# The unread matmuls of steps 8 to 20 in the chunk loop of a fused mLSTM and MoE kernel

## The chip, the core and the metric

The kernel runs on one core of one Trainium2 chip. The metric is the device time in microseconds (us); three runs of the kernel before gave 218.23, 218.18 and 217.78 us, median 218.18. The profile shown is of one further execution; its span, from the first to the last instruction, is 217.2 us.

Five engines work side by side. TensorE (PE in the profile; its weight loads are PEld) multiplies matrices into PSUM, VectorE (DVE), ScalarE (ACT) and GpSimd (POOL) do the rest of the arithmetic, and SyncE (SP) issues transfers. The clock of TensorE is granted by the chip and may fall to a half; the profile gives the granted share as PEclk.

## What is computed

Two stages, one behind the other. First an mLSTM cell over 4 x 8 heads, 768 time steps and a head size of 40. Then the result, 3072 rows of 320, goes through a mixture of 8 experts with one expert for each row.

```python
# stage 1, for each time step t
m_new = np.maximum(f_gate[:, :, t] + m, i_gate[:, :, t])
f_stab = np.exp(f_gate[:, :, t] + m - m_new)
i_stab = np.exp(i_gate[:, :, t] - m_new)
C = f_stab * C + i_stab * np.einsum('bhd,bhe->bhde', vt, kt)   # [..., None, None] cut
n = f_stab * n + i_stab * kt
h_tilde = np.einsum('bhde,bhe->bhd', C, qt)
denom = np.maximum(np.abs(np.einsum('bhd,bhd->bh', n, qt)), 1.0)
y[:, :, t] = sigmoid(o_gate[:, :, t]) * h_tilde / denom         # sigmoid written out in the reference

# stage 2, x: (3072, 320)
logits = x @ w_gate
expert_idx = np.argmax(logits, axis=1)
gate_w = probs[np.arange(N), expert_idx]                        # probs: softmax of logits
# rows sorted by expert; for each expert e
h = np.maximum(x_sorted[lo:hi] @ w1[e], 0.0)
y_sorted[lo:hi] = h @ w2[e]
out = gate_w[:, None] * y_sorted[inv_perm]
```

## The kernel before

The kernel turns the recurrence of stage 1 into chunks of 128 time steps: 4 batches of 6 chunks make NT = 24 steps of one loop, called the chunk loop here. While it runs, the rows that are done go through the gate of stage 2, are given a place and are sent to an array in HBM that is sorted by expert. Behind the loop the experts' multiplications run.

The order of instructions on each engine is the order of the program. One step of the loop, cut to the calls that matter:

```python
for s in range(-3, NT):
    P, odd = (s - 4) // 2, s % 2
    do(scores, s + 1)            # TensorE: scores of the next chunk
    do(transposes, s + 2)        # TensorE: k and q of the chunk after it
    ...
    do(values, s + 2)
    ...                          # a send; in even steps gate(P)
    do(states, s)                # TensorE: state times q, update of the state
    do(load, s + 6 if s >= -1 else -1)
    ...                          # in even steps rank(P, s - 1); warm(3) in the last
    do(xtrans, s - 1)            # TensorE: rows transposed for the gate
    do(ogate, s + 2)
    do(attend, s)                # TensorE: scores times values
    ...                          # place, keep_rows
    do(rows, s)                  # VectorE and GpSimd: x of this chunk
    if odd and 0 <= (s - 3) // 2:
        logits((s - 3) // 2, s - 1)      # TensorE: gate logits of two chunks
        choose((s - 3) // 2)             # VectorE: the expert of each row
        count((s - 3) // 2)
    ...                          # a send, a part of the constants, weight loads near the end
```

The change is in `scores`. Its s is the loop's step plus one. For each pair of heads there is one matmul into sA and one into sB; VectorE masks sA into dA, ScalarE copies sB to dB, GpSimd masks dB.

```python
def scores(s):
    d = st[s]
    kb, qb = d["kb"], d["qb"]
    sA = ps1.tile([128, PR, 128], F32, name="sA")
    sB = ps1.tile([128, PR, 128], F32, name="sB")
    for _ in range(3 if 1 <= s < 8 or s > NT - 4 else s % 2):
        nc.tensor.matmul(
            sA[:].rearrange("p j t -> p (j t)"), lhsT=ident_b[:],
            rhs=st[s - 1]["dA"][:].rearrange("p j t -> p (j t)"), start=True, stop=True,
        )
    for j in range(PR):
        nc.tensor.matmul(sA[:, j, :], lhsT=kb[0:D, j, :], rhs=qb[0:D, j, :], start=True, stop=True)
        nc.tensor.matmul(
            sB[:, j, :], lhsT=kb[DP : DP + D, j, :], rhs=qb[DP : DP + D, j, :], start=True, stop=True,
        )
    d["dA"] = chk.tile([128, PR, 128], BF16, name="dA")
    nc.vector.tensor_tensor(d["dA"][:], sA[:], cmask[:, None, :].to_broadcast([128, PR, 128]), op=ALU.mult)
    d["dB"] = chk.tile([128, PR, 128], BF16, name="dB")
    nc.scalar.copy(d["dB"][:], sB[:])
    ...                          # GpSimd: the lower half of dB to zero
```

The loop at the top of it issues matmuls whose result nobody reads: the identity times dA of the step before, 512 columns, into sA, which the score matmuls then overwrite. There are three of them in each of the s from 1 to 7 and from 21 to 23, and s % 2 in between. `warm` does the same into a tile named junk around the end of the loop.

The gate logits stand at the end of an odd step, so right ahead of the unread matmul of the next `scores`:

```python
def logits(P, host, c0=0):
    ...
    for i, t in enumerate(r["t"]):           # two chunks
        for db in range(DB):                 # three blocks of 128
            nc.tensor.matmul(
                lg[:, i * E : (i + 1) * E], lhsT=st[t]["xT"][:, db * 128 : (db + 1) * 128],
                rhs=wg_sb[:, db, :], ...     # E = 8 columns
            )
```

Behind the loop come `layer1` and `layer2` of the experts (hp and zp in the profile), their rows sent by GpSimd to the output (`out_dram`), with weights (`w_all`) that GpSimd's queue loads from HBM.

Of the kernel before, what the change touches and what calls it, by code (L numbers as in the profile page):

```python
# [19 lines left out]
def kernel(  # L20
# [22 lines left out]
    NT = N // 128  # L43
# [263 lines left out]
    with tc.tile_pool(name="ring", bufs=1) as ring_pool, \  # L307
# [67 lines left out]
        def scores(s):  # L375
            d = st[s]
            kb, qb = d["kb"], d["qb"]
            sA = ps1.tile([128, PR, 128], F32, name="sA")
            sB = ps1.tile([128, PR, 128], F32, name="sB")
            for _ in range(3 if 1 <= s < 8 or s > NT - 4 else s % 2):  # L380
                nc.tensor.matmul(  # L381
                    sA[:].rearrange("p j t -> p (j t)"), lhsT=ident_b[:],
                    rhs=st[s - 1]["dA"][:].rearrange("p j t -> p (j t)"), start=True, stop=True,
# [10 lines that stand above are left out]
            nc.gpsimd.affine_select(  # L394
                d["dB"][:], d["dB"][:], compare_op=ALU.is_ge, fill=0.0,
                base=0, pattern=[[0, PR], [1, 128]], channel_multiplier=-1,
            )
# [209 lines left out]
        for s in range(-3, NT):  # L607
            P, odd = (s - 4) // 2, s % 2
            last = s == NT - 1
            do(scores, s + 1)  # L610
            do(transposes, s + 2)
            if s == -3:
# [266 lines left out]
```

## Time and profile before

| What | Before |
|---|---|
| Time, median of three | 218.18 us |
| Span of the profiled execution | 217.2 us |
| Mean granted clock of TensorE | 0.984 |
| Chain that ended last, by engine | PE 46%, POOL 20%, issue 14%, DVE 9%, DMA 5%, ACT 3% |
| Line 381, all unread matmuls of `scores`, in the trace | 28 of 128x512 |
| Scores of the last chunk start | 110.6 us |

A row of a group or a timeline names the line of the kernel, the engine, the operation, what is written and read (out<-in) and the shape. In the chain of work that ended last, each row has a start in us, the time for which this piece held the chain, and the piece; "issue" there is time in which the engine waited for nothing that the profile shows. In the slices of the page each digit stands for one of 40 equal parts of the span, in tenths of busy time, or for PEclk in tenths of the full clock.

Some matmul records can be missing from a trace, and the ends of matmuls are modelled: a duration of one matmul is a latency which overlaps with its neighbours.

### The profile page before, as it was taken

Reading aid. Unit: us, or ns where it says so; the run is one execution under the profiler, and the core shown is the slowest. Engines: PE = TensorE matmul, PEld = TensorE weight load, DVE = VectorE, ACT = ScalarE, POOL = GpSimd, SP = SyncE. Lnnn points to the kernel's source line nnn. Section 1 sums busy time; section 2 is a strip of 40 time slices with the busy share of each in tenths; the row PEclk is TensorE's granted clock in tenths of the full one; section 3 lists DMA queues with packets and bytes.
Section 4 is the critical chain, followed back from the end, with each engine's and each line's share of the span. In section 5 each row is a group of like instructions: output and inputs, shape, how many; then the busy total and the mean of one; then the engine's idle time right before and its main releaser. Section 6 shows DMA issues by size and latency. Waiting matters only on the chain.

```text
span 217.2 us, 5727 instructions
## 1 busy us (share of the span) xinstructions
PE 192.3 (89%) x2048; PEld 151.8 (70%) x2057; DVE 124.8 (57%) x410; ACT 117.3 (54%) x273; POOL 139.3 (64%) x238
## 2 busy tenths in 40 slices
PE   1299999999999999979899998969999986999970
PEld 1168788899998899978786755647667654676740
DVE  7746667677787878797776342345833332333320
ACT  2458657797789897896751552323333322332330
POOL 6036786644869889749999489838656786253221
PEclk9999999999999999999998899999999999999996
DMA  7999999989999989994799999999999999985310
GB/s 139 197 198 190 205 205 204 231 156 254 178 193 173 195 161 206 193 204 84 142 184 262 222 205 150 193 254 233 216 229 245 231 290 408 409 317 201 149 46 10
DMA packets 120782, 44.32 MB, mean 204 GB/s; under 512 B 102506, under 2 KB 115821, under 8 KB 120752
## 3 DMA queue, kind: packets, MB, share of 16 engines
q1 hardware_dynamic: 105456, 25.34, 55.9%
q0 software_dynamic: 14832, 18.38, 40.3%
q8 instruction: 17, 0.28, 0.5%
q10 hardware_dynamic: 464, 0.21, 0.4%
q14 instruction: 13, 0.11, 0.2%
HBM read 39.30 MB, written 9.37 MB: 224 GB/s over the span
## 4 chain that ended last, share of the span: by engine, by line
PE 46%; POOL 20%; issue 14%; DVE 9%; DMA 5%; ACT 3%; POOLq 1%; ACTq 0%; DVEq 0%
POOL out_dram L287 7%; PE hp L474 6%; PE zp L280 5%; DMA w_all<-in_moe_w_dram 5%; PE hp L406 5%; PE tk L368 4%; POOL x_sorted L579 4%; PE dC L414 4%; PE hp L267 4%; PE tq L368 3%; PE xt L451 3%; PE sA L386 3%; PE sA L381 2%; POOL x_sb L444 2%; POOL rest L297 2%
## 5 line engine op out<-in xcount | busy, mean ns | idle before, releaser
L273 DVE TENSOR_SCALAR h<-hp 128x512 bf16<-128x512 f32 x25 | 17.3, 692 | 40.6 <-PE hp L267 26.3
L287 POOL DMA_INDIRECT out_dram<-zo,s_idx x20 | 20.0, 1002 | 16.3 <-ACT zo L285 10.0
L275 ACT ACTIVATE h<-hp 128x512 bf16<-128x512 f32 x25 | 14.9, 597 | 25.2 <-PE hp L267 19.9
L579 POOL DMA_INDIRECT x_sorted<-x_all,slots x24 | 25.3, 1054 | 4.9 <-issue 3.9
L444 POOL TENSOR_TENSOR x_sb<-x_sb,den 128x320 f32<-128x320 f32 x23 | 16.8, 729 | 17.2 <-DVE den L442 17.1
L280 PE MATMUL zp<-w_all,h 128*128 128x320 bf16 x160 | 24.5, 300 | 3.5 <-DMA w_all<-in_moe_w_dram 1.6
L280 PEld LDWEIGHTS <-h 128*128 128x128 bf16 x200 | 17.7, 98 | 13.2 <-DVE h L273 2.7
L285 ACT COPY zo<-zp 128x320 f32<-128x320 f32 x25 | 10.7, 426 | 27.2 <-PE zp L280 23.7
L267 PEld LDWEIGHTS <-w_all 128*128 128x128 bf16 x256 | 18.4, 98 | 5.6 <-issue 3.4
L393 ACT CAST dB<-sB 128x512 bf16<-128x512 f32 x24 | 14.0, 585 | 13.7 <-PE sB L387 11.5
L267 PE MATMUL hp<-xT,w_all 128*128 128x128 bf16 (+1 forms) x224 | 21.1, 243 | 0.0
L406 PE MATMUL hp<-C_sb,qT 104*128 104x82 f32 x160 | 20.7, 272 | 0.0
L368 PE MATMUL tk<-ident,kq 128*104 128x128 f32 x96 | 16.4, 296 | 4.2 <-DMA kq<-in_k_dram 4.2
L406 PEld LDWEIGHTS hp<-C_sb,qT 104*128 104x128 f32 x160 | 19.4, 192 | 0.3
L453 ACT COPY xT<-xt 128x384 f32<-128x384 f32 x24 | 11.6, 482 | 13.5 <-PE xt L451 12.5
L356 POOL CAST vAb<-vA 128x328 bf16<-128x328 f32 x24 | 11.0, 459 | 11.7 <-DVE vA L354 11.7
L474 PE MATMUL hp<-wg_sb,xT 128*128 128x8 f32 x144 | 18.0, 258 | 0.0
L414 PE MATMUL dC<-vA,kq 128*104 128x82 f32 x160 | 17.9, 254 | 0.0
L394 POOL TENSOR_SCALAR_AFFINE_SELECT dB<-dB 128x512 bf16<-128x512 bf16 x24 | 16.5, 689 | 1.7 <-ACT dB L393 1.5
L474 PEld LDWEIGHTS hp<-wg_sb,xT 128*128 128x128 f32 x144 | 17.4, 195 | 0.1
L391 DVE TENSOR_TENSOR dA<-sA,cmask 128x512 bf16<-128x512 f32 x24 | 16.0, 669 | 1.4 <-PE sB L387 1.4
L414 PEld LDWEIGHTS dC<-vA,kq 128*104 128x104 f32 x160 | 16.3, 172 | 0.0
(160 smaller groups left out, 455.8 us busy)
## 6 DMA issues: line engine op xcount, KB each, us to landing
wx<-w_all SPq DMA_DIRECT2D x10, 640.0 KB
w_all<-in_moe_w_dram POOLq DMA_DIRECT2D x8, 640.0 KB
w_all<-in_moe_w_dram POOLq DMA_DIRECT2D x8, 512.0 KB
kq<-in_k_dram SPq DMA_DIRECT2D x24, 160.0 KB
kq<-in_q_dram SPq DMA_DIRECT2D x24, 160.0 KB
v<-in_v_dram SPq DMA_DIRECT2D x24, 160.0 KB
o_sb<-in_o_gate_dram SPq DMA_DIRECT2D x24, 160.0 KB
x_sorted<-zrow POOLq DMA_DIRECT2D x8, 241.5 KB
```

The source lines that it names most:

```text
L267: nc.tensor.matmul(hp[:, i, :], lhsT=w[:, c : c + 128], rhs=xT[:, db, :], start=False, stop=(db == FL - 1), skip_group_check=True,)
L273: nc.vector.tensor_relu(dst, hp)
L280: nc.tensor.matmul(zp, lhsT=g["h"][:, fb, j * 128 : (j + 1) * 128], rhs=g["w"][1][:, fb, :], start=(fb == 0), stop=(fb == FB - 1),)
L287: ins = nc.gpsimd.indirect_dma_start(out=out[:, :], out_offset=bass.IndirectOffsetOnAxis(ap=at, axis=0), in_=zo, in_offset=None, bounds_ch ...
L368: nc.tensor.transpose(tp[:, j, :], two(d[n], j), ident[:])
L391: nc.vector.tensor_tensor(d["dA"][:], sA[:], cmask[:, None, :].to_broadcast([128, PR, 128]), op=ALU.mult)
L394: nc.gpsimd.affine_select(d["dB"][:], d["dB"][:], compare_op=ALU.is_ge, fill=0.0, base=0, pattern=[[0, PR], [1, 128]], channel_multiplier=-1,)
L406: nc.tensor.matmul(hp[:, 2 * j * D1 : (2 * j + 2) * D1], lhsT=d["qT"][:, j, :], rhs=st["C"][:, j].rearrange("p h d -> p (h d)"), start=(j ...
L414: nc.tensor.matmul(st["dC"][:, j], lhsT=two(d["k"], j), rhs=d["vA"][:, 2 * j : 2 * j + 2, :], start=(c == 0 and j == 0), stop=True, skip_g ...
L444: eng.tensor_tensor(x3d, x3d, den[:].unsqueeze(2).to_broadcast([128, H, D]), op=ALU.mult)
L474: nc.tensor.matmul(lg[:, i * E : (i + 1) * E], lhsT=st[t]["xT"][:, db * 128 : (db + 1) * 128], rhs=wg_sb[:, db, :], start=(fresh and i == ...
L579: ins = nc.gpsimd.indirect_dma_start(out=xs[:, :], out_offset=bass.IndirectOffsetOnAxis(ap=slots[:, t : t + 1], axis=0), in_=x_all[:, t, : ...
```

## The change

In the steps from s = 8 to s = 20, `scores` issues no unread matmul any more; before, it issued one where s is odd. The three of each earlier and later step stay, and so does `warm`. The unread matmuls have no part in the result. They keep TensorE occupied[...]; the change takes out those for which the loop's own work is to do that.

```diff
             sA = ps1.tile([128, PR, 128], F32, name="sA")
             sB = ps1.tile([128, PR, 128], F32, name="sB")
-            for _ in range(3 if 1 <= s < 8 or s > NT - 4 else s % 2):
+            for _ in range(3 if 1 <= s < 8 or s > NT - 4 else 0):
                 nc.tensor.matmul(
                     sA[:].rearrange("p j t -> p (j t)"), lhsT=ident_b[:],
                     rhs=st[s - 1]["dA"][:].rearrange("p j t -> p (j t)"), start=True, stop=True,
```

## The prediction

> **What bounds the kernel now.** I read the page first (busy shares, the slices, the chain that ended last), then the instructions of line 381, then the chain and the timeline of TensorE around each of the matmuls that go away. The page says that TensorE is the busiest engine, and the slices say where.
>
> ```profile
> PE 192.3 (89%) x2048; PEld 151.8 (70%) x2057; DVE 124.8 (57%) x410; ACT 117.3 (54%) x273; POOL 139.3 (64%) x238
> ...
> PE   1299999999999999979899998969999986999970
> ...
> PEclk9999999999999999999998899999999999999996
> ```
>
> One slice is 5.43 us. The chunk loop lies in slices 2 to 21, and TensorE is at nine tenths or more in nearly all of them until about 92 us, at full clock. So a matmul taken out of that stretch should shorten it, unless another engine sets the pace at that place. The clock row dips around slices 21 and 22 only.
>
> Which matmuls go? `scores(s)` runs one step ahead of the loop's counter. Before, its s from 8 to 20 gave s % 2 unread matmuls, so one each for s = 9, 11, 13, 15, 17, 19: six in all. The instructions of line 381 between 44 and 93 us are these six (the first row is their weight load):
>
> ```profile
> L381 PEld LDWEIGHTS <-ident_b x6: 181/181/181, 49.2 to 90.4; 128*128 128x128 bf16 x6
> L381 PE MATMUL sA<-dA,ident_b x6: 376/376/377, 49.3 to 90.5; 128*128 128x512 bf16 x6
> ```
>
> The 376 ns are a latency: they overlap with neighbours. What one costs on the path is read from the chain of work that ended last. At 82 us:
>
> ```profile
> 81.31 1.33 PE hp L474 x12
> 82.64 0.23 PE sA L381
> 82.87 0.16 PE sA L386
> ```
>
> The unread matmul holds the chain for 0.23 us. The chain shows the same 0.23 at 49.48, 58.07, 74.06 and 90.62 us. At 66 us it is different: there the chain leaves TensorE at the end of the gate logits and goes over VectorE.
>
> ```profile
> 64.59 1.34 PE hp L474 x12
> 65.94 0.02 issue
> 65.96 0.19 DVE lgs L484
> ...
> 66.98 0.43 DVE cums L498
> ...
> 67.62 0.60 DVE dA L391
> ```
>
> VectorE chooses experts until 67.62 us and only then makes dA, though its scores were in PSUM before 66.4 us. The unread matmul at 65.78 is in the shadow of that work.
>
> [...] the clock is half from 118.08 to 121.49 us (3.41 us) and falls again at 213.64, which is 28.0 windows after 118.08. [...] TensorE was busy for 3.05 us of the window before the fall.
> [...]
>
> So the six matmuls are there for the clock, not for a result: they stand right behind the twelve gate-logits matmuls (128 x 8 each, 1.33 us), which stream few columns.
>
> **The change, part by part.** It removes six weight loads and six 128x512 matmuls, and adds nothing. Apart from names, the instruction order of the engines stays. The wait for VectorE's last read of sA, which the unread matmul carried, moves to the first score weight load, beside its wait for kb on ScalarE: the form that the steps without an unread matmul have already.
> - Saving per place, a second way: with the unread matmul the first score matmul ends at 49.87 us, 0.39 after the last logits matmul (49.48). Where no unread matmul stands ahead of the scores (53.22 us), the first score matmul ends at 53.44, 0.16 after the matmul ahead of it (53.28). The difference is 0.23 us again.
> - On the path: five places, 5 x 0.23 = 1.15 us. The sixth, at 65.78, saves 0 by my reading (0.23 if I am wrong).
> - Does the saving last? Behind 90.62 us the chain goes over ACT (dB, 91.30), DVE and POOL, all started by these scores, so it moves with them. From 97.6 to 115 us it is POOL, which sends rows and issues weight loads one behind another (18.19 us busy in the 20 us from 96 to 116). That row of work begins with an x_sb at 96.71 that waited for the earlier chain, so it starts earlier too. Then comes the longest wait of all:
>
> ```profile
> 131.26 0.70 POOL w_all L178
> 131.96 1.00 POOL w_all L183 x2
> ...
> 133.01 11.71 DMA w_all<-in_moe_w_dram
> ```
>
>   The transfers queue up behind those issued earlier. But in 100 to 104 us the DMA engines are busy for only 0.38, so the queue that makes this wait begins after that, with issues from POOL's row, and moves with it. I count the whole 1.15 us through to the end.
> - Sum without a clock effect: 218.18 - 1.15 = 217.03 us.
>
> **The rivals.**
>
> *The clock falls.* This is the real danger, since the matmuls are there to prevent it. To judge it I counted streamed columns in each 3.41 us window as the trace has them: every matmul but transposes, f32 columns counted four times, a matmul across an edge by its part[...]. Counting f32 four times is my choice; counted once, a window that kept its clock (70.29 to 73.70) would lie below one that lost it. Two windows were followed by a fall: 114.66 to 118.08, and the last with matmuls in it, 210.24 to 213.65. Their non-transpose groups:
>
> ```profile
> L474 PE MATMUL hp<-wg_sb,xT 128*128 128x8 f32 x12 | 1.5, 256 | 0.0
> L567 PE MATMUL junk<-dA,ident_b 128*128 128x512 bf16 x2 | 0.9, 440 | 0.0
> ```
>
>   With eight 41-column matmuls and 0.8 of an unread one inside, the first has 384 + 328 + about 400 columns, 0.14. The last has 5.3 matmuls of 320 columns, 0.21. Both fell. The windows that kept the clock in the chunk loop have 0.34 and more; one of the lowest, 80.53 to 83.94, has 0.35 with one unread matmul (0.06) in it, so about 0.29 without. Sliding the window over the trace from 40 to 92 us[...] the lowest share is 0.27 before, and 0.24 with the six taken out and what follows pulled forward. The other minima move up as often as down, for what is pulled forward into the window is f32 work. So the limit is somewhere from 0.21 to 0.34, and the change moves the worst place by 0.03. [...] At 120.88 us twelve logits matmuls with 0.61 us of their time at half clock took 1.70 us instead of 1.49, a third of the slow time lost, so about 1.2 us for a whole window. One fall would cancel the gain (218.2), two would make 219.4. For it speaks the purpose of the lines; against it, that steps without an unread matmul keep the full clock already (70.29 to 73.70 has eleven of twelve logits matmuls and none of line 381). I give one extra fall or more a quarter.
>
> *Another engine paces those steps.* If VectorE, ScalarE or GpSimd were the bound at more of the places, as at 66 us, the gain would shrink to 0.5 us or less (217.7). From 76 to 92 us GpSimd is busy for about 1.8 of each 2 us, so it is near. Against it: the chain itself passes through line 381 at five of six places.
>
> *The transfer hides it.* If the 11.71 us wait for w_all ended by the DMA queue's own work, begun early, the end would not move: 218.1. The idle DMA time at 100 to 104 speaks against it. One chance in ten.
>
> **Range and chances.** 217.0 with three chances in five, something from 217.5 to 218.2 where part of it is hidden or one fall happens, and about 219 with two falls: I put the middle at 217.1 us. The three times before span 0.45 us, which I add below, and a fall with a little scatter above: 216.3 to 218.7. A gain of 2% would need 4.4 us, more than the six matmuls' whole latency (2.3 us); a loss of 2% would need at least four falls. Chances: faster by over 2% 0.01, within 2% 0.97, slower by over 2% 0.02.
>
> **What would show it right or wrong.** In the profile after: no line 381 from 44 to 93 us; the first score matmul ends 0.16 us after the last logits matmul, not 0.39; the logits groups in the loop start 0.23 us earlier per place, except over the one at 66 us, and by 90 us by about 0.9 us in all; GpSimd's row of sends and the wait for w_all start 1.1 us earlier. A half-clock stretch between 40 and 100 us, with 1.2 us lost behind it, proves the clock rival; a loop that ends earlier while the multiplications of the experts start no earlier proves the transfer rival. I am wrong altogether if the time rises without a fall of the clock.

## The result and the profile after

The changed kernel took 0.9941 of the time before (95% interval 0.9916 to 0.9967): on a median of 218.03 us before, that is 1.3 us less (0.7 to 1.8), with executions at 216.54 and 216.92 us. This ratio, like those below, leaves out executions that lie more than about 1.5% above the fastest of the same kernel: here two of the four, at 222.95 and 221.82 us with a mean TensorE clock of 0.945 instead of 0.975. By an estimate from clock and span, 2 x (1 - 0.945) x 221.2 us, the longer of the two spent 24 us at half clock, 14 more than the one at 216.54 us. That is four windows of 3.41 us more, at 1.6 us each; no trace shows where they lay.

The page of the changed kernel, in the rows that were shown of the one before:

```profile
PE 193.0 (90%) x2051; PEld 153.2 (71%) x2051; DVE 125.5 (58%) x410; ACT 117.5 (55%) x273; POOL 138.8 (65%) x238
...
PE   1289999999999899999998999898999999999970
...
PEclk9999999999999999969999699999999999999996
```

TensorE is as full as before, and the clock row has a second dip, in the slice that begins at 91 us. The stretches around it say how long it was:

```profile
core 0: us, PE busy (x) PEld busy (x) DVE busy (x) ACT busy (x) POOL busy (x), PEclk, DMA share, GB/s
88.41:91.82 3.41, 3.18 (x39) 2.89 (x39) 2.46 (x9) 2.77 (x7) 3.23 (x6) 1.00 0.84 153
91.82:95.24 3.42, 3.42 (x28) 3.33 (x27) 2.90 (x10) 2.64 (x9) 2.34 (x5) 0.50 1.11 205
```

One window of 3.41 us at half clock, right behind the scores that once had an unread matmul ahead of them (s = 19). "Window" here and below is the spacing that the two profiles show: from the first full clock to the last fall it changes only after whole multiples of 3.413 us. It was full for 102.40 and 92.16 us in the profile before (30 and 27 windows) and for 75.09, 23.89 and 88.75 us in the one after (22, 7 and 26), and half for one window at each fall between them. The chain at the place near 66 us, of which the prediction said that VectorE paced it:

```profile
64.58 1.33 PE hp L474 x12
65.91 0.16 PE sA L386
...
66.36 0.58 ACT dB L393
66.94 0.49 ACT kb L370
67.43 0.49 ACT qb L370
67.92 0.49 ACT qT L373
68.41 0.58 ACT gex L513 x4
...
69.01 0.17 DVE gsum L517
```

No line 381 stands between logits and scores any more. And it is ScalarE, started by these scores, on whose last piece (gex) VectorE waits.

These two profiles don't show where the gain comes from. The spans are 217.2 and 214.7 us, yet the copies of the first expert rows (lines 285, 273) run later in the one after, by 1.4 us: its full clock began at 16.73 us instead of 15.68, it lost 0.9 us at one tq transpose (70.64 us) and it had the window above. Near the loop's end it also waited for a load of the output gate, which landed 9.55 us after its issue, where none in the profile before took over 5.2 us:

```profile
101.60 9.55 DMA o_sb<-in_o_gate_dram
```

ScalarE stood still for the last 1.7 us of it, and by the last steps of the loop this cost 0.8 us (measured on x_sb against the second profile of the change, below: 1.70 us later ahead of the wait, 2.50 behind it). The lead of the profile after comes from 176 us on, where in the profile before TensorE stood still for reasons that the trace doesn't name:

```profile
177.22 2.20 PE L280 MATMUL zp<-w_all,h 128*128 128x320 bf16 x14 [0.80 <-issue]
...
181.66 0.22 PE L242 MATMUL tp<-ident_b,x_all 128*64 128x128 bf16 x1 [0.48 <-issue]
182.60 0.27 PE L239 MATMUL tp<-ident_b,x_all 128*128 128x128 bf16 x2 [0.72 <-issue]
```

The change touches nothing there. A pair of profiles without such accidents comes first among the experiments.

### The profile page after: what moved, and what is told of

Its sections match the earlier page's. It is cut to its first block, busy times and chain, and to the rows that moved or that the text cites. A ratio compares the mean times of both kernels' runs of the same rounds, so it can differ in the third digit from the quotient of the medians.

```text
span 214.7 us, 5730 instructions
## 1 busy us (share of the span) xinstructions
PE 193.0 (90%) x2051; PEld 153.2 (71%) x2051; DVE 125.5 (58%) x410; ACT 117.5 (55%) x273; POOL 138.8 (65%) x238
## 4 chain that ended last, share of the span: by engine, by line
PE 62%; DVE 10%; issue 9%; POOL 7%; ACT 5%; DMA 4%; POOLq 0%; DVEq 0%; ACTq 0%
PE zp L280 9%; PE hp L267 8%; PE hp L474 7%; PE hp L406 5%; PE dC L414 5%; DMA o_sb<-in_o_gate_dram 4%; PE tk L368 4%; POOL out_dram L287 4%; PE tq L368 4%; PE xt L451 4%; PE hp L258 3%; PE sA L386 3%; PE sA L381 3%; PE hp L280 2%; PE hp L426 2%
## 5 line engine op out<-in xcount | busy, mean ns | idle before, releaser
L414 PE MATMUL dC<-vA,kq 128*104 128x82 f32 x160 | 18.5, 261 | 0.0
L414 PEld LDWEIGHTS dC<-vA,kq 128*104 128x104 f32 x160 | 17.1, 178 | 0.0
```

The costliest lines, as they stand in the source:

```text
L414: nc.tensor.matmul(st["dC"][:, j], lhsT=two(d["k"], j), rhs=d["vA"][:, 2 * j : 2 * j + 2, :], start=(c == 0 and j == 0), stop=True, skip_g ...
```

## The experiments

They ran on three chips, in groups: the first four kernels, the next four, the last four. The kernel before ran beside each group, with medians of 216.24, 222.81 and 224.70 us, so ratios are compared and not times. Ratios are to the kernel before on the same chip. "Path theory" below means that the six matmuls leave the path and nothing else happens; "clock theory", that they hold the clock, and that windows at half clock come where they go.

### The kernel before again, and the change again

No edit in the first; the second is the change itself.

> The kernel before, unchanged, as a measure of what changes without any change. Clock theory (the unread matmuls hold the clock): every execution near 218.0 us, mean granted clock 0.98, at most one half-clock window between 16 and 211 us. Chance theory (windows at half clock fall to either kernel alike): some executions at a mean clock of 0.95 and 221 us here too.

> The changed kernel again. Path theory (six matmuls of 0.23 us leave the path, nothing else): 216.6 us, mean clock as before, 0.98. Clock theory: the executions differ with the number of half-clock windows, about 1.5 us for each: near 216.7 us at a mean clock of 0.975 and near 222 us at 0.945, and the trace shows half-clock windows between 40 and 100 us.

Measured: ratios 0.9996 (0.9964 to 1.0029) and 0.9934 (0.9899 to 0.9969). Neither trace has a half-clock window between 17 and 146 us, so here the two loops can be laid side by side. The shift of ScalarE's copy of sB into dB, which follows at once on the scores, against the kernel before (0.12 us of earlier start taken off):

| Place | s = 9 | 11 | 13 | 15 | 17 | 19 |
|---|---|---|---|---|---|---|
| Shift of dB, us | -0.23 | -0.46 | -0.70 | -0.93 | -1.16 | -1.18 |

The rows of s = 13, of the kernel before and of the changed one:

```profile
67.15 0.59 ACT L393 CAST dB<-sB 128x512 bf16<-128x512 f32 x1 [0.47 <-PE sB L387]
66.33 0.59 ACT L393 CAST dB<-sB 128x512 bf16<-128x512 f32 x1 [0.23 <-PE sB L387]
```

Up to s = 17 each place gives its 0.23 us, that at 66 us (s = 13) too. By s = 19 what s = 17 gave is gone again. There the chain goes over VectorE, and here is what holds VectorE, in the changed kernel:

```profile
82.48 1.18 DVE L491 SCALAR_TENSOR_TENSOR sc<-lgs,lmin,first_w 128x8 f32<-128x8 f32 x2
82.88 0.73 POOL L444 TENSOR_TENSOR x_sb<-x_sb,den 128x320 f32<-128x320 f32 x1
83.69 0.17 DVE L496 TENSOR_REDUCE mx<-sc 128x2 f32<-128x16 f32 x1
```

The two small operations on sc take 1.18 us where they take 0.36 at 66 us, and end with GpSimd's x_sb at 83.61. The x_sb of the last step but one in the loop starts at 113.46 us instead of 114.77: 1.31 less 0.12, so the loop gained 1.19 us. The shift is still 1.32 us at 140 us. Behind that the two profiles part by 3 us more, as the wait for w_all ended otherwise (below). The two profiles of the kernel before part by 3.05 us there as well, so this isn't shown to be the change's.

The clock theory's windows between 40 and 100 us are not in this trace, and the mean clock over all executions was 0.986, against 0.984 of the kernel before on the chip. So far the path theory holds alone.

### Three instead of one

```diff
-            for _ in range(3 if 1 <= s < 8 or s > NT - 4 else s % 2):
+            for _ in range(3 if 1 <= s < 8 or s > NT - 4 else 3 * (s % 2)):
```

> Three unread matmuls instead of one in each odd s from 9 to 19. Path theory: 12 more of 0.23 us [...] on the path, 218.0 + 2.6 = 220.6 us. Clock theory: no half-clock window between 16 and 110 us in any execution, so all executions within 0.3% of each other, at 220.6 us or a little less. If VectorE or ScalarE pace the steps, the matmuls fill idle time of TensorE and the time stays below 219.5 us.

Measured: ratio 1.0141 (1.0093 to 1.0189), 3.0 us more. In the trace dB shifts by 0.43 us per place against the kernel before, 2.58 us after all six: what two more matmuls of 0.215 us make. So the price of an unread matmul is right, at every place, s = 17 too; the loop's own clock stayed full (the first fall came at 122.04 us). The executions still spread from 218.05 to 219.99 us, 0.9%: more than the 0.3% that the clock theory gave them.

### None in the loop

```diff
-            for _ in range(3 if 1 <= s < 8 or s > NT - 4 else s % 2):
+            for _ in range(0):
```

> No unread matmuls in any step of the loop (those of the first seven and last three steps are left out too; the five of the loop's end stay). Path theory: 28 recorded matmuls of 0.21 to 0.23 us fewer than before, of them about 20 on the path: 218.0 - 4.5 = 213.5 us. Clock theory: half-clock windows all over the loop, each about 1.5 us; four of them cancel the gain, so 215 to 222 us and a mean clock under 0.97.

Measured: ratio 0.9841 (0.9786 to 0.9896), 3.4 us less. The full clock came at 21.90 us instead of 16.93, which put the fourth step 1.3 us behind the kernel before; by 111.7 us it was 3.3 us ahead; then came half clock from 114.06 to 124.30 us, three windows, and at 126 us nothing was left of the lead. The 3.7 us by which this profile is shorter at its end all came behind 142 us, at the wait for w_all, so it doesn't show where the ratio's gain comes from. Between 22 and 114 us no window fell. So in this trace the middle kept the clock without unread matmuls. At the start the full clock came later than in any other trace (15.68 to 18.88 us). At the end the kernels that keep them lose the clock too: one window from 118.08 us in the first profile before, two from 122.04 with three instead of one. That the unread matmuls are worth their time at the ends isn't shown: the kernel without any in the loop had the lower ratio (0.9841 against the change's 0.9934).

### Five at one place

```diff
-            for _ in range(3 if 1 <= s < 8 or s > NT - 4 else 0):
+            for _ in range(3 if 1 <= s < 8 or s > NT - 4 else 5 if s == 13 else 0):
```

and the same with 17 for 13; the line taken out is that of the changed kernel.

> The changed kernel with five unread matmuls in s = 13 and none in the other steps from 8 to 20. Five hold TensorE for 0.23 + 4 x 0.215 = 1.09 us. The prediction's reading (VectorE choosing experts paces this step, the matmuls are in its shadow): the masked scores dA of the step and the x_sb of the steps behind start no later than in the changed kernel, measured from the step before. Rival (ScalarE's row of copies, which starts with these scores, paces it): they start 1.1 us later.

> The same with the five in s = 17, where the trace of the changed kernel shows the chain going over VectorE. Shadow theory: the first 0.2 us are hidden and x_sb of the steps behind starts 0.8 to 0.9 us later than in the changed kernel. If nothing hides them: 1.1 us, as at s = 13 by the rival.

Measured in the traces, x_sb against the changed kernel's: at s = 13 it goes from 0.76 us later (67.30 to 68.06) to 1.85 (70.82 to 72.67), so all 1.09 us arrive. At s = 17 it goes from 2.31 (82.88 to 85.19) to 2.56 (87.03 to 89.59): 0.25 us arrive and 0.84 are hidden. (The offsets ahead of these are other waits earlier in the runs.) The prediction's shadow exists, but at s = 17 and not at s = 13. The 0.84 is mostly this run's own: already ahead of the five, at 67.57 and 76.09 us, VectorE's two operations on sc took 1.51 and 1.43 us instead of 0.36, and put VectorE's side of the loop 2.31 us later, where the scores of s = 15 were only 1.65 later. By this estimate 0.66 us of the shadow come from there, and about 0.2 us are left for an undisturbed loop. That is what I expected, and it agrees with the table, where s = 17 lost its 0.23 us, and with three matmuls instead of one, where the two more at s = 17 were not hidden.

### The change a third time

> The changed kernel once more. If windows at half clock come more often with the change, its mean clock lies below that of the kernel before on this chip and some executions are 5 us longer; if they come alike, the mean clocks agree within 0.005 and the ratio is 0.993.

Measured: ratio 0.9962 (0.9907 to 1.0018), so no gain is clear of noise here; mean clock 0.976 against 0.974 of the kernel before. On average the clock is no worse with the change on this chip or the last, though it was in the change's first four executions (0.960, against 0.984 in the profile before). But this trace has what the clock theory speaks of: half clock from 49.89 to 53.30 us. The chain there:

```profile
48.20 1.33 PE hp L474 x12
49.53 0.16 PE sA L386
...
49.86 0.97 PE tk L368 x4
50.83 0.85 PE tq L368 x4
51.68 1.63 PE hp L406 x8
```

In the changed kernel's trace with full clock the same three last rows hold the chain for 0.58, 0.44 and 0.85 us. The difference is 1.58 us, and the steps behind are 1.64 us later: so much did this fall cost, at a place where TensorE paces. TensorE was busy for 3.34 of the 3.41 us of the window before the fall. In the changed kernel's first profile the fall at 91.82 us cost only 0.44 us (the shift against the other trace of the change goes from 1.24 to 1.68), for there TensorE doesn't pace: in the trace with full clock the chain runs over VectorE from 89.92 to 95.67 us, but for one matmul.

### Unread matmuls at the two ends alone

```diff
-            for _ in range(3 if 1 <= s < 8 or s > NT - 4 else s % 2):
+            for _ in range(3 if 1 <= s < 3 or s > NT - 4 else 0):
```

> Unread matmuls only in s = 1, 2 and 21 to 23: three each; none from 3 to 20. Path theory: 15 matmuls of 0.215 us fewer than in the changed kernel, 2 to 3 us off the loop, so 213.5 us with the before of the same chip at 216.2 (ratio 0.987). Clock theory as the prediction had it (each matmul guards its window): half-clock windows between 25 and 100 us, and no gain over the changed kernel. The kernel without any in the loop kept the full clock from 21.9 to 114 us, which speaks for the first.

> Unread matmuls in s = 1, 2 and 21 to 23 alone, once more, beside the kernel with three more places on the same chip: ratio to before 0.98 to 0.987, that is 2.1 us for the ten fewer in s = 3 to 7 not hidden plus 1.2 for those from 9 to 19.

Measured: 0.9827 (0.973 to 0.9924) on the second chip, 1.0014 (0.9922 to 1.0107) on the third. The hope of 0.98 held once. These ratios rest on two and three executions; the means over all are 219.56 against 222.28 us on the second chip and 226.74 against 224.90 on the third. The trace of the second one shows a wait that neither kernel has had, first among TensorE's waits from 25 to 116 us:

```profile
PE tq L368 <- DMA kq<-in_q_dram: 1.1, 1, 1.1
```

The loop has become fast enough to reach a q that hasn't landed. TensorE idles for 1.1 us at 48 to 49 us, and the clock is at half from 48.57 to 55.40 us, two windows. The wait needn't be what cost the clock: of the window that ended at 48.57 us it took only 0.4 us. The first of the two has the same wait at 68.3 us (1.26 us), TensorE was busy for 2.07 us of the window around it (66.67 to 70.08), and the clock stayed full; it fell at 90.56 us, after a window without idle time. What the matmuls in s = 3 to 7 took was partly time that the loads needed.

### The ends and three places

```diff
-            for _ in range(3 if 1 <= s < 8 or s > NT - 4 else s % 2):
+            for _ in range(3 if 1 <= s < 3 or s > NT - 4 else int(s in (9, 15, 19))):
```

> Unread matmuls: three each in s = 1, 2 and 21 to 23, as in the kernel with the first two and the end, and one each in s = 9, 15 and 19, where by my count of the windows a fall is most likely (falls were seen there at 49.9, 90.6 and 91.8 us). Cost: 3 x 0.23 = 0.7 us in each execution. If a fall in the loop costs 1.6 us and these prevent one in every two or three executions, the mean is about equal to that of the kernel without them and the mean clock higher by 0.002; ratio to before 0.983 to 0.988.

Measured: 0.998 (0.9925 to 1.0035), mean clock 0.951, against 0.950 without the three and 0.964 of the kernel before. A miss: the three matmuls neither raised the clock by more than 0.001 nor could the time show their price. Its trace, too, waits for q (1.3 us) and falls at 49.07 us, with the unread matmul of s = 9 in the window. One unread matmul did not save this window, in which TensorE was busy for 2.90 of 3.41 us.

### A stretch of narrow matmuls and one of transposes

```diff
+            if P == 4:
+                for i in range(60):
+                    nc.tensor.matmul(
+                        st[host]["hp"][:, 496:504], lhsT=st[r["t"][0]]["xT"][:, 0:128],
+                        rhs=wg_sb[:, 0, :], start=False, stop=True, skip_group_check=True,
+                    )
             for i, t in enumerate(r["t"]):       # the logits of step 11
```

> The changed kernel with 60 more matmuls of 8 columns (the shape of the gate logits, f32, unread, into columns that nobody reads) ahead of the logits of step 11: with those, 72 x 0.111 = 8 us in which TensorE is never idle and streams few columns. If what holds the clock is streamed columns (my reading of the windows that fell), the clock falls inside this stretch whatever the phase, at the end of the first whole 3.41 us window in it, and the loop ends later by 6.7 us plus the slower matmuls, 9 us or more. If it is that TensorE is busy at all, no window falls and the loop ends 6.7 us later.

Measured: the clock fell at 67.81 us and stayed at half for 27.3 us, eight windows. (The trace has 120 matmuls: an f32 matmul of this kernel appears as two, which is also why the six of the logits appear as twelve.) The stretches before and after the fall:

```profile
64.40:67.81 3.41, 3.41 (x36) 3.41 (x33) 0.93 (x4) 1.68 (x4) 3.19 (x6) 1.00 0.87 162
67.81:71.22 3.41, 3.41 (x18) 3.41 (x18) 0.00 (x0) 0.00 (x0) 1.24 (x3) 0.50 1.00 180
```

TensorE is busy for the whole of the first window, in weight loads too, and the clock falls at its end. The matmuls then take 0.187 us each instead of 0.111. The loop ended 26.1 us later: 13.3 for 120 matmuls at full clock, and 12.8 for eight windows, 1.6 each.

The other stretch is of transposes, in the changed kernel:

```diff
-                for j in range(PR):
+                for j in [0, 1, 2, 3] * (13 if s == 13 and n == "k" else 1):
                     nc.tensor.transpose(tp[:, j, :], two(d[n], j), ident[:])
```

> The changed kernel with the four k transposes of one step done 13 times (128 columns, f32, each pass overwriting the same tile): 56 transposes at 0.142 us in a row, 8 us. If transposes do not count for the clock, [...] the clock falls inside the stretch as in the kernel with the narrow matmuls, and they take longer than 0.142 us each. My count of ten traces' windows says that they do count: then no window falls between 55 and 75 us and the loop ends 48 x 0.142 = 6.8 us later.

Measured:

```profile
62.78 5.88 PE L368 MATMUL tk<-ident,kq 128*104 128x128 f32 x52
```

The clock stayed full, from 18.2 to 188.9 us. The 48 more transposes cost 5.2 us (0.11 each in a row; my 0.142 was that of four and their start). They fill 3.2 us of the window from 62.59 to 66.01 us, and the clock was at 1.00 in the next window too: these f32 transposes held a clock that was full. Whether such transposes bring it up wasn't tried. The 8-column matmuls of the other stretch did not hold it, with TensorE busy for 3.41 of 3.41 us. What the clock follows was not shown.

## Why the prediction held, point by point

- **The price of one, 0.23 us.** Right: 0.23 at each place, and 0.215 for each further one.
- **Five of six on the path, 1.15 us.** The sum was right (1.19), but one of its terms was not. The step that failed is the reading of the chain at 65.94 us: it shows VectorE's choosing of experts, and I took it for the pace. The same chain has 0.74 us of "issue" at 68.63, ahead of gsum, which I passed over:

```profile
68.22 0.41 DVE vA L354
68.63 0.74 issue
69.36 0.17 DVE gsum L517
```

  That was VectorE waiting for ScalarE's gex, as the profile after names it. So ScalarE paced, the scores start ScalarE, and the saving arrived. The hidden place was s = 17, where I had put 0.23 us on the path because the chain ran through line 381. Two errors of 0.23 cancelled, and that was luck.
- **The saving lasts to the end.** To about 140 us it does (1.32 with the earlier start). Beyond, it can't be seen in single profiles: the wait for w_all held the chain for 11.71 us in the first profile before, 10.91 in the second, 10.00 in the change's second. The ratios (0.9941, 0.9934, 0.9962) fit a gain of 1.2 us. The means over all executions don't show it: 215.95 us with the change against 216.09 on the first group's chip (a difference of 0.1 +- 0.7 us), 221.61 against 222.28 on the second's (0.7 +- 1.2), and 219.56 against 218.02 where the change was first run, four executions each. So the gain is shown for the loop and for the shorter executions; how much of it an average execution keeps stays open.
- **The transfer hides it.** Open for w_all, whose landing differs more between two profiles of the kernel before than the change is worth. Another load did take part of the gain in one of the change's three profiles: the output gate, 0.8 us at the loop's end. When more was taken out, the loop waited for q too.
- **The clock falls.** Falls do come in the loop with the change: at 49.89 and 91.82 us, at two of the six places. That the matmuls taken out would have prevented them was my estimate and isn't shown. My count by which I judged the danger was wrong. (A share of 1 in it is about 8100 columns: 3.41 us at the 0.215 us from one unread matmul of 512 columns to the next, 22.38 to 22.60 us in the profile before.) By it the window that fell at 49.89 had a share of 0.57 and one that held (67.93 to 71.34 us, same kernel) had 0.25, outside my bracket of 0.21 to 0.34. It gave narrow f32 matmuls four times their columns and transposes nothing, which no trace had shown. In the two stretches a window filled with 8-column matmuls for 3.41 us lost the clock, and one with 3.2 us of f32 transposes kept it. The cost was set too low: 1.6 us and not 1.2 where TensorE paces, and 0.44 where it doesn't. How much more often windows fall in the loop with the change stays open: of the three traces with unread matmuls at all six places none has a fall between 22 and 110 us, and of the ten that lack some or all of the six (without the one with narrow matmuls) five have, two of the change's three among them. The mean clocks agree on two chips; where the change was first run, two of its four executions had about four windows more than the other two.
- **217.1 us.** The executions in the ratio lay at 216.5 to 216.9, a little under the middle and inside the range, though the profiled one had a fall (0.44 us) and the wait for the output gate. The two others lie above the range; they had about four windows more at half clock, as many as the prediction had named for a loss of 2%.

Leaving out the unread matmuls of the whole loop gave 0.984 beside the change's 0.993, on the one chip where it ran. Leaving them at both ends alone gave 0.983 beside 0.996, but on the third chip, where the change itself did not run, it gained nothing.

## What to carry to other kernels

An unread matmul that is meant to keep the clock has a price that can be read from the chain (here 0.23 us) and a worth that one profile didn't show here, as the windows lay differently over the kernel in each: the full clock began at 15.68 us in the profile before and at 16.73 in the one after. It came later without such matmuls at the start of the loop (21.90 us). Inside the loop a fall came only now and then and cost up to 1.6 us, and whether their price is well spent there, or at its end, stayed open. A stretch of "issue" in the chain is to be asked what it waited for before its engine is called the pace. And each wait taken out brings the next transfer nearer: past some point the loop reaches its loads and idles, as it did for q here (1.1 to 1.3 us).

## What the runs showed that I had not expected

- Full busy time did not hold the clock: 3.41 of 3.41 us busy with 8-column matmuls, and it fell; f32 transposes in a row held it for 5.9 us, and a window with only 2.07 us of busy time held it too.
- Two VectorE operations of 8 columns took 1.18 us instead of 0.36 beside a GpSimd operation on x_sb (0.73 us), and ended within 0.05 us of it (83.66 and 83.61 us). Why they slow down was not shown.
- The chips differed more than the kernels did: medians of the kernel before of 216.24, 222.81 and 224.70 us, with mean clocks of 0.984, 0.974 and 0.964.
